# Delta-rule attention and two MLPs on one core: a reordered triangular solve on VectorE, a third high-word buffer, and a later first coupling in the second group

## The chip, the cores and the metric

One core of a Trainium2 chip runs the whole program. The metric is the device time of one execution in microseconds (us). Five engines take their own instruction queues in order: TensorE (PE in the rows, PEld for its weight loads), VectorE (DVE), ScalarE (ACT), GpSimd (POOL), and SyncE (SP), which here only issues DMA transfers. Engines meet through semaphores; an instruction whose wait is not fulfilled holds everything behind it on its own engine.

## The reference, cut to what matters

Attention is a recurrence with a state of 48 x 48 for each of 32 pairs of batch and head; behind it stand two MLPs on the same 4 x 768 tokens.

```python
def _attn_ref(q, k, v, beta):              # (4, 8, 768, 48) each, beta without the last axis
    k_n = k / (norm(k, axis=-1, keepdims=True) + 1e-06)
    for t in range(S):                     # S = 768
        y[:, :, t] = q[:, :, t] @ state
        v_old = state^T k_n[:, :, t]
        state = state + beta_t * outer(k_n[:, :, t], v[:, :, t] - v_old)

def _moe_ref(x, w_in, g_ln, w_sg, b_sg, w_out):
    h = gelu(x @ w_in)                     # 384 -> 1024
    u, v = h[..., :512], h[..., 512:]
    v_n = layernorm(v) * g_ln
    v_s = einsum('ts,bsd->btd', w_sg, v_n) + b_sg[None, :, None]
    return x + (u * v_s) @ w_out

def _moe2_ref(x, mu_k, mu_r, w_k, w_v, w_r):
    xk, xr = mixes of x and the token before
    return sigmoid(xr @ w_r) * (relu(xk @ w_k)**2 @ w_v)
```

## The kernel before

**Chunks and groups.** The 768 tokens are cut into 12 chunks (`s`) of 64, and two chunks make one of six groups (`g`, counted from 0). Inside a chunk the recurrence becomes a triangular system. PE makes the products of the keys with each other (`gram`), VectorE inverts the two 32 x 32 diagonal blocks of all 32 (chunk, pair) systems of a group at once (`solver(g)`, lanes are partitions), and PE makes from the inverses `DT` and the block under the diagonal `GL` the coupling of the two halves (`couple(g, k)`, one call for each chunk k of the group).

**The steps of a chunk** run on PE in two halves `o` of the pairs: `st_rq` (keys times state), `residual` (values minus that; ACT in group 0, VectorE in all others), `st_d` (the residual times the inverses `DT`, into `rk`), `st_n` (its product, copied as `u1`, times the coupled `GL`), `st_s` (state), `st_y` (output). `st_d` needs the solve and the residual; only `st_n` needs the coupling. Each half-chunk is one slot, each slot has three ticks, a group has 24 ticks.

**The solve** is one chain on VectorE: a transpose, a reciprocal norm (some 20 small instructions), the scaling of four 8 x 8 blocks (L389), a forward substitution inside the 8 x 8 blocks (pairs of a product, L355, and a sum, L393), the joining of 8 x 8 blocks to 16 x 16, and of these to 32 x 32 (again products of 256 to 1024 elements for a partition, each followed by its sum), and a transpose into `DT` (L440). Every product writes the same scratch tile `tmp`, so a product waits for the sum before it, and the sum for the product. `solver(g + 1)` runs while group g is on PE; the next one starts when the group changes.

**Weights in two words.** `w_in`, `w_out` and `w_k` are split into a high and a low word by `narrow` jobs: four VectorE instructions for each piece (L169, L171, L173, L175, on tiles `na` and `raw`), then POOL L177, an ACT copy L120 (the high word), POOL L123 (the low word). A new piece's L169 waits until an `na` buffer is free, which is after L123 of the piece that had it; there are `NNA` = 2 of them.

**What sets the order.** A planner in Python deals out VectorE's work at each tick (`background`) among three kinds: layer norm, solve, jobs, in the ratio `SHARE` (row 1 of the table is for group 0). PE, ACT, VectorE and POOL run the order in which the code is written; PE fills time with matmuls on a tile `warm` (L726) and with the input projection of the MLP (`v_units` L635, `u_units` L687). SP's order is set by the framework. Once the attention is through, PE goes on with the spatial mix (L960) and the products behind it (L151); `begin_early` loads `w_sg` for that mix in pairs of blocks ahead of time, one of them into a staging tile `stw`, through which later pieces of `w_sg` also pass.

Of the kernel before, what the change touches and what calls it, by code (L numbers as in the profile page):

```python
# [7 lines left out]
F32 = mybir.dt.float32  # L8
# [4 lines left out]
ALU = mybir.AluOpType  # L13
# [47 lines left out]
SHARE = ((1, 12, 1), (1, 4, 1), (2, 8, 2))  # L61
NRAW = 3
NNA = 2
# [23 lines left out]
def fused_kernel(  # L87
# [161 lines left out]
    with ExitStack() as at:  # L249
# [101 lines left out]
        def product(a_off, a_dims, a_t, b_off, b_dims, b_t):  # L351

            sh = [d[1] for d in a_dims]
            tv = vw(tmp, 0, [(sh[1] * sh[2], sh[0]), (sh[2], sh[1]), (1, sh[2])])
            V.tensor_tensor(tv, vw(a_t, a_off, a_dims), vw(b_t, b_off, b_dims), op=ALU.mult)  # L355
            return tv, sh[0] * sh[1] * sh[2] / 960 + 0.16

        def solver(g):
# [28 lines left out]
            for m in range(4):  # L387
                blk = NT[:, 8 * m:8 * m + 8, 8 * m:8 * m + 8]
                V.tensor_tensor(blk, blk, vw(c, 8 * m, [(1, 8), (0, 8)]), op=ALU.mult)  # L389
                yield 0.15  # L390
# [5 lines left out]
            for i in range(1, 8):  # L396
# [7 lines left out]
            yield 0.3  # L404
            for dst in (0, 1):
                for p in range(2):
                    o = 16 * p
                    if dst == 0:
                        tv, t = product(32 * (o + 8) + o, [(32, 8), (0, 8), (1, 8)], NT,
                                        128 * p, [(0, 8), (8, 8), (1, 8)], Yt)  # L410
                        ov = vw(NT, 8 + 528 * p, [(1, 8), (32, 8)])
                    else:
                        tv, t = product(33 * (o + 8), [(32, 8), (0, 8), (1, 8)], Dm,
                                        8 + 528 * p, [(0, 8), (32, 8), (1, 8)], NT)
                        ov = vw(Dm, 32 * (o + 8) + o, [(32, 8), (1, 8)])
                    yield t
                    yield total(ov, tv, t)
                    if dst and p == 0:
                        V.tensor_copy(vw(NT, 24, [(1, 8), (32, 8)]), ov)
                        yield 0.2  # L420
            for last in (0, 1):
                if last == 0:
                    ops = [(vw(Yt, 16 * j, [(1, 16), (16, 4)]),
                            (32 * 16 + j, [(32, 16), (0, 4), (1, 16 - j)], NT,
                             16 + 33 * j, [(0, 16), (32, 4), (1, 16 - j)], NT))
                           for j in (12, 8, 4, 0)]
                else:
                    ops = [(vw(Dm, 32 * (16 + i), [(32, 4), (1, 16)]),
# [824 lines left out]
```

## Time and profile before

| | us |
|---|---|
| median of 3 runs | 744.63 (743.13 to 745.2) |
| the profiled execution, time | 746.13 |
| its span | 744.3 |
| PE busy | 689.7 (93%) |
| VectorE busy | 506.3 (68%) |
| ACT busy | 364.8 (49%) |
| POOL busy | 202.5 (27%) |

The span is the time between the first and the last record; some 1.8 us lie around it. The page's chain of waits, followed back from the end, gives PE 67% of the span and VectorE 20%; of VectorE's part the largest lines are L355 (products of the solve, 5%) and L393 (their sums, 3% and 2%). TensorE's granted clock has a mean of 0.975 of full speed; in the rows 1.00 is 2.4 GHz and 0.50 is 1.2 GHz.

### The profile page before, as it was taken

What the parts mean: (1) busy time and instruction counts of PE and PEld (TensorE: products, weight loads), DVE (VectorE), ACT (ScalarE), POOL (GpSimd) and SP (SyncE); (2) the same over time, 40 slices, a digit from 0 to 9 for tenths busy, and PEclk for the clock granted to TensorE, in tenths of its full rate; (3) what the DMA queues carried; (4) which work ended last, traced back from release to release, by engine and by line L of the source; (5) the groups of instructions that cost most, each with busy time, mean ns of one, the idle gap of its engine ahead of it and who ended that gap; (6) DMA issues with size and microseconds to landing.
All of it is one profiled execution on the core that took longest, in us unless ns stands there. A gap on an engine that the chain in (4) does not pass through costs nothing.

```text
span 744.3 us, 24530 instructions
## 1 busy us (share of the span) xinstructions
PE 689.7 (93%) x10688; PEld 622.4 (84%) x10688; DVE 506.3 (68%) x1014; ACT 364.8 (49%) x696; POOL 202.5 (27%) x253
## 2 busy tenths in 40 slices
PE   3459789998998999899999999999999999999998
PEld 3337568887886987779999999998989899999997
DVE  5989999897888796642566857598656464736251
ACT  3226656776676676774331413146445453626140
POOL 3033544454345255463131515330000000000000
PEclk9968989999999899999999999999999999999999
DMA  8502443675556566848763545259000000000000
GB/s 237 133 29 86 126 102 94 165 215 160 138 178 165 148 182 172 231 144 226 245 222 106 168 153 168 85 193 232 23 21 22 22 21 22 11 33 11 32 11 33
DMA packets 81547, 88.72 MB, mean 119 GB/s; under 512 B 24704, under 2 KB 64320, under 8 KB 81440
## 3 DMA queue, kind: packets, MB, share of 16 engines
q1 hardware_dynamic: 76384, 77.72, 35.3%
q0 software_dynamic: 5056, 9.44, 4.8%
q8 instruction: 84, 1.38, 0.7%
q14 instruction: 23, 0.19, 0.1%
HBM read 56.60 MB, written 25.82 MB: 111 GB/s over the span
## 4 chain that ended last, share of the span: by engine, by line
PE 67%; DVE 20%; issue 4%; DMA 4%; POOL 2%; ACT 2%; SPq 0%; POOLq 0%; ACTq 0%; DVEq 0%
PE ms L151 34%; PE ms L960 11%; PE ms L687 5%; DVE sg L355 5%; PE ms L635 4%; DVE sg L393 3%; PE ms L563 2%; PE ms L456 2%; PE sps L549 2%; DVE Yt L393 2%; PE rk L521 1%; PE ms L333 1%; PE rk L534 1%; PE rk L498 1%; DMA raw<-in_w_k_dram 1%
## 5 line engine op out<-in xcount | busy, mean ns | idle before, releaser
L151 PE MATMUL ms<-wvh,sl 128*128 128x384 f32 x192 | 64.7, 337 | 0.5 <-DVE sl L123 0.5
L151 PE MATMUL ms<-wvh,sh 128*128 128x384 f32 x192 | 64.6, 337 | 0.1
L151 PE MATMUL ms<-wvl,sh 128*128 128x384 f32 x192 | 64.5, 336 | 0.0
L1059 ACT ACTIVATE gh<-w 128x384 fp32r<-128x384 f32 x32 | 16.8, 526 | 93.8 <-DVE w L1058 93.8
L177 POOL TENSOR_TENSOR na<-na,raw 128x256 int32<-128x256 int32 (+2 forms) x43 | 35.9, 835 | 96.2 <-ACT gh L1059 40.7
L151 PE MATMUL ms<-xm_hi,sw0h 128*128 128x512 f32 x144 | 56.1, 390 | 0.0
L151 PE MATMUL ms<-xm_hi,sw0l 128*128 128x512 f32 x144 | 56.1, 389 | 0.0
L151 PE MATMUL ms<-xm_lo,sw0h 128*128 128x512 f32 x144 | 56.0, 389 | 0.0
L123 DVE TENSOR_TENSOR sl<-sg,sh 128x512 fp32r<-128x512 f32 x48 | 33.2, 692 | 28.8 <-ACT sh L120 28.7
L960 PE MATMUL ms<-sw0h,g 128*128 128x384 f32 x192 | 50.2, 335 | 0.0
L960 PE MATMUL ms<-ws1h,g 128*128 128x384 f32 x192 | 49.9, 334 | 0.0
L120 ACT ACTIVATE sh<-sg 128x512 fp32r<-128x512 f32 x48 | 30.3, 631 | 34.0 <-DVE sg L1172 34.0
L1189 DVE TENSOR_TENSOR sg<-sg,ms 128x384 f32<-128x384 f32 x24 | 13.3, 553 | 49.3 <-PE ms L151 49.3
L355 DVE TENSOR_TENSOR sg<-sg,Yt 128x512 f32<-128x512 f32 (+10 forms) x78 | 45.6, 584 | 1.7
L514 POOL TENSOR_SCALAR_AFFINE_SELECT SQ<-SQ 64x512 f32<-64x512 f32 x36 | 27.9, 774 | 50.2 <-ACT SQ L513 49.0
L1171 ACT ACTIVATE sg<-ms 128x512 f32<-128x512 f32 x48 | 28.6, 595 | 26.1 <-PE ms L151 24.1
L1172 DVE TENSOR_TENSOR sg<-sg 128x512 f32<-128x512 f32 x48 | 33.2, 692 | 10.8 <-ACT sg L1171 10.8
L687 PE MATMUL ms<-xl,wiu_hi 128*128 128x256 f32 x144 | 39.5, 296 | 0.0
L687 PE MATMUL ms<-xh,wiu_hi 128*128 128x256 f32 x144 | 38.4, 289 | 0.8 <-issue 0.8
L687 PE MATMUL ms<-xh,wiu_lo 128*128 128x256 f32 x144 | 38.5, 290 | 0.0
L151 PEld LDWEIGHTS ms<-wvh,sl 128*128 128x128 f32 x192 | 36.1, 188 | 0.8 <-DVE sl L123 0.8
L393 DVE TENSOR_REDUCE sg<-sg 128x64 f32<-128x512 f32 (+3 forms) x48 | 35.9, 748 | 0.9
(246 smaller groups left out, 2155.5 us busy)
## 6 DMA issues: line engine op xcount, KB each, us to landing
u_d<-ug SPq DMA_DIRECT2D x24, 256.0 KB, 3.9
u<-u_d SPq DMA_DIRECT2D x16, 384.0 KB, 4.9
vn_d<-v SPq DMA_DIRECT2D x22, 256.0 KB, 3.3
vk<-in_vk_dram SPq DMA_DIRECT2D x24, 192.0 KB, 3.7
vk<-in_vk_dram SPq DMA_DIRECT2D x12, 384.0 KB, 4.5
out_dram<-sg SPq DMA_DIRECT2D x24, 192.0 KB, 1.9
kT<-in_kt_d_dram SPq DMA_DIRECT2D x8, 512.0 KB, 4.5
SQ<-in_q_d_dram SPq DMA_DIRECT2D x36, 96.0 KB, 3.6
```

What stands on the lines that cost most here:

```text
L120: A.activation(hi, src, AF.Copy)
L123: eng_lo.tensor_tensor(lo, src, hi.bitcast(F32), op=ALU.subtract)
L151: T.matmul(pt, lhsT=a, rhs=b, start=(i == 0), stop=(i == n - 1))
L177: G.tensor_tensor(a.bitcast(I32), a.bitcast(I32), w_lo.bitcast(I32), op=ALU.add)
L355: V.tensor_tensor(tv, vw(a_t, a_off, a_dims), vw(b_t, b_off, b_dims), op=ALU.mult)
L393: V.tensor_reduce(out=o_ap, in_=tv, axis=AX.X, op=ALU.add)
L514: G.affine_select(out=pt, in_=pt, pattern=[[0, 8], [1, C]], compare_op=ALU.is_gt, fill=0.0, base=0, channel_multiplier=-1)
L635: T.matmul(vstat[g, b], lhsT=a[:, c], rhs=w[:, c], start=first, stop=last)
L687: T.matmul(vstat["u"][:, 2 * P * d:2 * P * d + 2 * P], lhsT=w[:, c, ds_], rhs=a[:, c].rearrange("p b t -> p (b t)"), start=first, stop=last)
L960: T.matmul(pt[:, :DM], lhsT=v[:, ds_], rhs=w, start=(c == 0 and i == 0), stop=(c == 5 and i == 2))
L1171: A.activation(r, pt, AF.Relu)
L1172: V.tensor_tensor(r, r, r, op=ALU.mult)
```

## The change

Five things are changed.

1. **The solve's instructions.** The four scalings become one of 4 x 8 x 8; the first substitution step, which sums one element, becomes one product without a sum; the joins take two or three products and their sums in turn, in separate parts of `tmp` (offset `at`).
2. **The second group's couplings** are put at tick 27 and 33 or later: behind `st_d`, `st_s` and `st_y` of the slot in which the first one stood ahead.
3. **The second solve** (during group 0) starts at tick 0 instead of 1, and gets 8 parts to 1 of the jobs' instead of 4 to 1.
4. **`NNA`** is 3.
5. **The tile `stw`** is gone, which makes room for the third `na`: pair 1 of `w_sg` is loaded into the key buffer `kTb[2]`, and the first later piece passes through a tile `st0` of the mix's own pool.

```diff
-SHARE = ((1, 12, 1), (1, 4, 1), (2, 8, 2))
+SHARE = ((1, 12, 1), (1, 8, 1), (2, 8, 2))
-NNA = 2
+NNA = 3
...
-        def product(a_off, a_dims, a_t, b_off, b_dims, b_t):
+        def product(a_off, a_dims, a_t, b_off, b_dims, b_t, at=0):
-            tv = vw(tmp, 0, [(sh[1] * sh[2], sh[0]), (sh[2], sh[1]), (1, sh[2])])
+            tv = vw(tmp, at, [(sh[1] * sh[2], sh[0]), (sh[2], sh[1]), (1, sh[2])])
...
-            for m in range(4):
-                blk = NT[:, 8 * m:8 * m + 8, 8 * m:8 * m + 8]
-                V.tensor_tensor(blk, blk, vw(c, 8 * m, [(1, 8), (0, 8)]), op=ALU.mult)
-                yield 0.15
+            blk = vw(NT, 0, [(264, 4), (32, 8), (1, 8)])
+            V.tensor_tensor(blk, blk, vw(c, 0, [(8, 4), (1, 8), (0, 8)]), op=ALU.mult)
+            yield 0.4
+            V.tensor_tensor(vw(Yt, 1, [(64, 4)]), vw(NT, 32, [(264, 4)]), vw(Yt, 0, [(64, 4)]),
+                            op=ALU.mult)
+            yield 0.15
...
-            for i in range(1, 8):
+            for i in range(2, 8):
...
+            def pairs(ops, hooks={}):
+
+                for k, (x, e) in enumerate(ops):
+                    ov, args, at = e
+                    if x == "*":
+                        tvs[at], t = product(*args, at=at)
+                        yield t
+                    else:
+                        yield total(ov, tvs[at], 0.16 + args[1][0][1] * args[1][1][1] * args[1][2][1] / 960)
+                    if k in hooks:
+                        hooks[k]()
...
+                yield from pairs([("*", es[0]), ("*", es[1]), ("+", es[0]), ("+", es[1])])
...
+                    yield from pairs([("*", a), ("+", a), ("*", b), ("*", d), ("+", b), ("*", c_),
+                                      ("+", d), ("+", c_)])
...
+                    yield from pairs([("*", c_), ("*", d), ("+", c_), ("*", b), ("+", d), ("+", b),
+                                      ("*", a), ("+", a)], hooks)
...
                 p += -p % 6 if p % 6 > 2 else 0
+                if g == 1:
+                    p = max(p, 27)
                 for k in range(2):
                     later.append((p + 6 * k, lambda k=k: couple(g, k)))
...
-                streams.append([point[0] + SOLVE0, solver(g + 1), "solve"])
+                streams.append([point[0] + (SOLVE0 if g else 0), solver(g + 1), "solve"])
...
-                  1: fetch_pair(stg.tile([P, 2, DM], F32, name="stw", bufs=1), 1)}
+                  1: fetch_pair(vw(kTb[2], 0, [(DM, 2), (1, DM)]), 1)}
...
-                    st[2] = fetch_pair(stg.tile([P, 2, DM], F32, name="stw", bufs=1), 2)
+                    st[2] = fetch_pair(st[1], 2)
...
-    sts += [(stg, "stw"), (vr, "st1"), (vr, "st2")]
+    sts += [(vr, "st0"), (vr, "st1"), (vr, "st2")]
```

How this moves instructions is not told by the diff alone. In the rows below the line numbers of after are some 2 to 17 higher (L393 is L395, L440 is L455, L475 is L492, L456 is L473, L521 is L538, L726 is L743).

VectorE, from the end of the first solve to the start of the second: `sw0l` is the first solve's `DT`, `m_sb` a small constant. Before:

```order
L440 STREAM_TRANSPOSE sw0l_115<-sg_110 128x32x32
L175 SCALAR_TENSOR_TENSOR na<-raw,na 128x256
L827 TENSOR_SCALAR m_sb<-mu_sb 128x6
L169 TENSOR_SCALAR na<-raw 128x256 x2
L171 TENSOR_SCALAR na<-na 128x256 x2
L173 TENSOR_SCALAR na<-na 128x256 x2
L360 STREAM_TRANSPOSE sg_108<-sg_109 128x1024
```

And after, from the last product of the first solve on:

```order
L355 TENSOR_TENSOR sg_111<-sg_110,Yt 128x1024
L175 SCALAR_TENSOR_TENSOR na<-raw,na 128x256
L395 TENSOR_REDUCE sg_110<-sg_111 128x4x16
L455 STREAM_TRANSPOSE sw0l_115<-sg_110 128x32x32
L175 SCALAR_TENSOR_TENSOR na<-raw,na 128x256
L844 TENSOR_SCALAR m_sb<-mu_sb 128x6
L360 STREAM_TRANSPOSE sg_108<-sg_109 128x1024
```

Six instructions of two pieces have left the place between the two solves. Inside the second solve stand 12 instructions of pieces instead of 21.

VectorE, from the end of the second solve (`DT`) over the second group's first residual (`r`) to the third solve (L360). Before:

```order
L440 STREAM_TRANSPOSE DT<-sg_110 128x32x32
L169 TENSOR_SCALAR na<-raw 128x256
L175 SCALAR_TENSOR_TENSOR na<-raw,na 128x256
L475 TENSOR_TENSOR r_1642<-vk,rk 128x384
L171 TENSOR_SCALAR na<-na 128x256
L173 TENSOR_SCALAR na<-na 128x256
L175 SCALAR_TENSOR_TENSOR na<-raw,na 128x256
L360 STREAM_TRANSPOSE sg_108<-sg_109 128x1024
```

After, from the fourth instruction behind the transpose `L455 ... DT` on (the first three are L175, L171, L173):

```order
L175 SCALAR_TENSOR_TENSOR na<-raw,na 128x256
L169 TENSOR_SCALAR na<-raw 128x256 x2
L171 TENSOR_SCALAR na<-na 128x256 x2
L173 TENSOR_SCALAR na<-na 128x256 x2
L492 TENSOR_TENSOR r_1626<-vk,rk 128x384
L175 SCALAR_TENSOR_TENSOR na<-raw,na 128x256 x2
L169 TENSOR_SCALAR na<-raw 128x256
L171 TENSOR_SCALAR na<-na 128x256
L173 TENSOR_SCALAR na<-na 128x256
L360 STREAM_TRANSPOSE sg_108<-sg_109 128x1024
```

Between the transpose and the residual stand 14 instructions of pieces where there were two, and five more stand between the residual and the third solve, where there were three.

PE at the start of group 1. Before, the coupling (L456) stands ahead of `st_d` (L521):

```order
L726 MATMUL ms<-warm 128x512
L456 MATMUL ms<-DT,sw0h_113 32x32 x32
L726 LDWEIGHTS warm
...
L521 MATMUL rk<-r_1642,DT 32x48 x32
L549 MATMUL sps_104<-SQ_127,vk 48x48
```

After, `st_d` (L538), `st_s` (L566) and `st_y` (L580) come first, and `st_n` (L551) follows the coupling (L473):

```order
L743 MATMUL ms<-warm 128x512
L538 MATMUL rk<-r_1626,DT 32x48 x32
L566 MATMUL sps_104<-SQ_127,vk 48x48
...
L743 MATMUL ms<-warm 128x512
L473 MATMUL ms<-DT,sw0h_113 32x32 x32
L743 LDWEIGHTS warm
...
L551 MATMUL rk<-u_1731,sw0h_113 32x48 x16
```

The number of matmuls is the same. On SP the loads of `raw` have moved too: the last piece of `w_in` is now loaded behind six stores of attention output (`xT<-yst`, L600 and L605):

```order
L605 DMA xT<-yst 32x2x128
L160 DMA raw<-in_w_in_dram 128x512
L279 DMA SQ_127<-in_q_d_dram 48x8x64
L279 DMA SQ_128<-in_q_d_dram 48x8x64
L273 DMA vk<-in_vk_dram 64x768
```

Before, two pieces of `w_out` stood there:

```order
L588 DMA xT<-yst 32x2x128
L160 DMA raw<-in_w_out_dram 128x384 x2
L273 DMA vk<-in_vk_dram 64x768
L279 DMA SQ_127<-in_q_d_dram 48x8x64
L279 DMA SQ_128<-in_q_d_dram 48x8x64
```

That piece's L169 is the one that stands between the residual and the third solve.

## Rows read from the trace of the kernel before

**Rows 1.** Busy time by engine, 340 us to the end: PE, PEld, DVE, ACT, POOL, clock.

```profile
340.00:744.00 404.00, 400.28 (x2172) 380.80 (x2170) 233.58 (x400) 157.30 (x283) 54.24 (x55) 1.00 0.30 92
```

**Rows 2.** Waits of PE: total us, times, longest.

```profile
PE ms L726 <- DVE warm L435: 8.4, 1, 8.4
...
PE ms L456 <- DVE na L169: 4.7, 1, 4.7
PE ms L456 <- DVE sw0l L440: 3.8, 2, 3.6
```

**Rows 3.** Timeline of PE: start, duration, line, count, idle time before and releaser.

```profile
96.07 1.92 PE L456 MATMUL ms<-DT,sw0h 32*32 32x32 f32 x64 [4.70 <-DVE na L169]
...
104.65 0.87 PE L534 MATMUL rk<-u,sw0h 32*32 32x48 f32 x32
...
192.46 1.20 PE L456 MATMUL ms<-DT,sg 32*32 32x32 f32 x64 [1.56 <-DVE DT L440]
```

**Rows 4.** Busy time by engine behind the 4.70 us wait; the clock is 0.50.

```profile
96.00:102.50 6.50, 6.43 (x164) 4.89 (x164) 6.05 (x20) 2.50 (x5) 3.40 (x5) 0.50 0.27 73
```

**Rows 5.** Timeline of VectorE in the first solve.

```profile
22.42 0.49 DVE L389 TENSOR_TENSOR sg<-sg,c 128x64 f32<-128x64 f32 x3
...
29.08 0.69 DVE L355 TENSOR_TENSOR sg<-sg,Yt 128x512 f32<-128x512 f32 x1
29.80 0.69 DVE L393 TENSOR_REDUCE sg<-sg 128x64 f32<-128x512 f32 x1
30.41 0.28 DVE L171 TENSOR_SCALAR na<-na 128x256 f32<-128x256 f32 x1
...
33.59 0.42 DVE L355 TENSOR_TENSOR sg<-sg 128x256 f32<-128x256 f32 x1
```

**Rows 6.** Timeline of VectorE between the first and the second solve.

```profile
49.56 0.40 DVE L175 SCALAR_TENSOR_TENSOR na<-raw,na 128x256 uint32<-128x256 uint32 x1
...
52.09 0.29 DVE L169 TENSOR_SCALAR na<-raw 128x256 uint32<-128x256 uint32 x1 [1.88 <-POOL wiv_lo L123]
...
54.04 1.23 DVE L360 STREAM_TRANSPOSE sg<-sg 128x1024 f32<-128x1024 f32 x1
```

**Rows 7.** Timeline of VectorE behind the second solve, and the third solve's start.

```profile
95.77 0.28 DVE L169 TENSOR_SCALAR na<-raw 128x256 uint32<-128x256 uint32 x1
...
98.09 1.24 DVE L360 STREAM_TRANSPOSE sg<-sg 128x1024 f32<-128x1024 f32 x1
```

**Rows 8.** Groups of VectorE in the second solve: busy us and mean ns.

```profile
L169 DVE TENSOR_SCALAR na<-raw 128x256 uint32<-128x256 uint32 x5 | 3.0, 592 | 0.0
...
L173 DVE TENSOR_SCALAR na<-na 128x256 uint32<-128x256 uint32 x6 | 1.9, 324 | 0.0
```

**Rows 9.** Timeline of POOL: one piece and the start of the next.

```profile
96.50 0.73 POOL L177 TENSOR_TENSOR na<-na,raw 128x256 int32<-128x256 int32 x1 [1.84 <-issue]
...
98.72 0.73 POOL L177 TENSOR_TENSOR na<-na,raw 128x256 int32<-128x256 int32 x1
```

**Rows 10.** Timeline of VectorE: the last residual of group 1.

```profile
133.45 0.56 DVE L475 TENSOR_TENSOR r<-vk,rk 128x384 f32<-128x384 f32 x1 [2.14 <-PE qk L501]
```

**Rows 11.** Timeline of SP's queue, and landing times of the loads of `raw`.

```profile
92.56 1.30 SPq L583 DMA_DIRECT2D xT<-yst  x2
93.92 2.63 SPq L588 DMA_DIRECT2D xT<-yst  x4
...
DMA to landing us min/median/max: 2.4/2.9/4.0
```

**Rows 12.** ACT, PE and SP's queue behind the attention, and a load's landing time.

```profile
343.11 0.60 ACT L644 ACTIVATE v<-ms 128x512 f32<-128x512 f32 x1 [4.84 <-PE ms L635]
...
349.26 0.86 PE L635 MATMUL ms<-wiv_hi,xh 128*128 128x512 f32 x3
...
341.50 0.90 SPq L243 DMA_DIRECT2D st<-in_w_sg_dram  x2
...
st<-in_w_sg_dram SPq DMA_DIRECT2D x2, 192.0 KB, 4.3
```

More of the change, by code (lines that the diff above doesn't have):

```diff
@@ L404, in solver @@
             yield 0.3
+            def pairs(ops, hooks={}):
[8 more added lines that the diff above has]
+                        hooks[k]()
+            tvs = {}
             for dst in (0, 1):
+                es = []
                 for p in range(2):
@@ L416, in solver @@
[L416 to L420, printed above, removed]
+                        es.append((vw(NT, 8 + 528 * p, [(1, 8), (32, 8)]),
+                                   (32 * (o + 8) + o, [(32, 8), (0, 8), (1, 8)], NT,
+                                    128 * p, [(0, 8), (8, 8), (1, 8)], Yt), 512 * p))
+                    else:
+                        es.append((vw(Dm, 32 * (o + 8) + o, [(32, 8), (1, 8)]),
+                                   (33 * (o + 8), [(32, 8), (0, 8), (1, 8)], Dm,
+                                    8 + 528 * p, [(0, 8), (32, 8), (1, 8)], NT), 512 * p))
@@ L421, in solver @@
+                yield from pairs([("*", es[0]), ("*", es[1]), ("+", es[0]), ("+", es[1])])
+            V.tensor_copy(vw(NT, 24, [(1, 8), (32, 8)]), es[0][0])
+            yield 0.2
             for last in (0, 1):
                 if last == 0:
[L423 to L426, printed above, removed]
-                else:
-                    ops = [(vw(Dm, 32 * (16 + i), [(32, 4), (1, 16)]),
-                            (32 * (16 + i) + 16, [(32, 4), (0, 16), (1, i + 4)], Dm,
-                             0, [(0, 4), (16, 16), (1, i + 4)], Yt)) for i in (0, 4, 8, 12)]
@@ L431, in solver @@
-                for i, (ov, args) in enumerate(ops):
-                    tv, t = product(*args)
-                    yield t
-                    if g == 0 and last and i == 1:
-                        V.memset(warm, 0.0)
-                    if g == 0 and last and i == 2:
-                        scale_v(0)
-                    yield total(ov, tv, t)
+                    es = [(vw(Yt, 16 * j, [(1, 16), (16, 4)]),
+                           (32 * 16 + j, [(32, 16), (0, 4), (1, 16 - j)], NT,
+                            16 + 33 * j, [(0, 16), (32, 4), (1, 16 - j)], NT), at)
+                          for j, at in ((0, 0), (4, 0), (12, 768), (8, 0))]
@@ new lines, in solver @@
+                    a, b, d, c_ = es
+                    yield from pairs([("*", a), ("+", a), ("*", b), ("*", d), ("+", b), ("*", c_),
+                                      ("+", d), ("+", c_)])
+                else:
+                    es = [(vw(Dm, 32 * (16 + i), [(32, 4), (1, 16)]),
+                           (32 * (16 + i) + 16, [(32, 4), (0, 16), (1, i + 4)], Dm,
+                            0, [(0, 4), (16, 16), (1, i + 4)], Yt), at)
+                          for i, at in ((4, 0), (0, 768), (8, 0), (12, 0))]
+                    c_, d, b, a = es
+                    hooks = {2: lambda: V.memset(warm, 0.0), 3: lambda: scale_v(0)} if g == 0 else {}
+                    yield from pairs([("*", c_), ("*", d), ("+", c_), ("*", b), ("+", d), ("+", b),
+                                      ("*", a), ("+", a)], hooks)
```

6 lines of the change are left out of this document (removed).

## The prediction, made blind

> **What bounds the kernel now.** I read the busy times by stretch first. From 340 us on PE is busy 400.28 of 404.00 us at full clock [rows 1], and the change touches little there: what is saved ahead of 340 us should arrive at the end nearly whole. So I read PE's waits ahead of 340 us next. The long ones are for VectorE's solves: 8.4 us ahead of the first solve's end, 4.7 us at the coupling of group 1 behind the second, and 3.8 us in two waits behind a later one, 3.6 of them in one [rows 2]. The timeline shows the 4.7 us wait ending at 96.07, with the product `st_n` it was for at 104.65, and a third such wait of 1.56 us at 192.46 [rows 3]. Behind the 4.7 us wait the granted clock is 0.50, which is 1.2 GHz: the coupling there takes 1.92 us and in rows 3 also 1.20 [rows 3, 4]. So this wait costs more than itself.
>
> **The first solve (whole on the path).** The row to read is how soon the next instruction starts. A product of 512 elements at 29.08 is followed by its sum, which waits for it, after 0.72 us; the sum at 29.80 is followed by an instruction that does not wait after 0.61 [rows 5]. A direct wait costs 0.11 us. Behind the substitution, the code before has 18 instructions that wait for the one directly ahead of them, the code after 5: 13 x 0.11 = 1.4 us. Three of four scalings, at some 0.13 us each, make way for longer work of 256 elements: a tile operation of that size is busy 0.42 us [rows 5], less an overlap of 0.09 with the next, so 0.5 becomes 0.3; the sum that falls away and the two direct waits beside it I take for 0.3, an estimate from the small instructions in these rows. Together 1.9 to 2.0 us.
>
> Against this stands a rule of the Trainium skill (VectorE: DVE Perf Modes, The DRAIN you can't avoid): every VectorE operation is followed by a flush of its pipeline, which ordering or leaving out semaphores does not save. By that the 1.4 us would not be there and the first solve would give 0.5. Rows 5 speak for 0.11 a pair; what the rule would make of the time is rival 3.
>
> **The second solve.** Its start moves from 54.04 to about 48.0: the instruction behind the first solve, at 49.56, comes 2.0 earlier, and six instructions of pieces with their 1.88 us wait for POOL no longer stand ahead of L360 [rows 6]. Its length was 95.77 - 54.04 = 41.7 us [rows 6, 7]. It loses nine instructions of pieces. The means of these in that stretch are 0.324 to 0.592 us [rows 8]; less 0.09 overlap that is 2.1 to 4.5, and I take 3.8, near the upper end since what falls away is work that VectorE and POOL did at the same time. Its own instructions save only 0.7, since pieces already stood between many of its pairs (36 direct waits before, 32 after). So it ends at about 48.0 + 41.7 - 4.5 = 85.2, with bounds of 83.5 and 87 against 95.8.
>
> **What is late next: the residual.** The coupling no longer waits; `st_d` needs the residual, and 14 instructions of pieces now stand ahead of that on VectorE. At 0.3 us each they take 4.3. But the last two L169 need `na` buffers that POOL frees, and POOL takes 2.2 us from one piece to the next (96.50 to 98.72) [rows 9]; two such pieces, behind the 0.4 us of the first L175, make the second buffer free at about 4.8 us behind the solve, and five more instructions follow. So the residual starts 6.2 us behind the solve (bounds 4.3 and 7.2), at 91.4, and is through at 91.9. PE comes to that place 4.7 us ahead of 96.07, at 91.4, less the 2.0 of the first solve, so at 89.4 [rows 3]. It waits about 2.5 us there: the old wait is halved, not gone.
>
> From `st_d` to `st_n` stand the pieces that stood from the coupling to `st_n` before, in another order: 104.65 - 96.07 = 8.6 us at half clock. At full clock I take 6.2 (8.6 less 6.5 us of rows 4 at a saving of 0.72 of 1.92). A wait of 1.56 us was followed by a lower clock in part, so I take 7.0. `st_n` then starts at 91.9 + 7.0 = 98.9 instead of 104.65: **5.7 us**, with bounds of 2.5 and 9.
>
> **What takes part of it back: the third solve.** It starts at 98.09 now [rows 7]. The last piece of `w_in` stands ahead of it, and its load now stands on SP behind six stores of output, 1.30 + 2.63 us of issuing [rows 11]. These wait for an ACT copy that stands behind another piece; I put its end at 89.1, so the load is issued at 93.1, lands after 2.4 to 4.0 us, median 2.9 [rows 11], and three instructions later the third solve starts at 96.9 (bounds 95 and 98.5), 1.2 us earlier. Up to group 1's last residual it saves some 0.7 of its own time. There VectorE waited 2.14 us for PE [rows 10]. So VectorE can follow PE by 1.2 + 0.7 + 2.14 = 4.0 us, not by 5.7. Some tenths of slack lie between that residual and its user on PE. I take **4.2 us** for groups 0 and 1.
>
> **The later groups.** From group 2 on, only VectorE's work behind the last residual counts, since ahead of it VectorE waits for PE as at 133.45. Counting the instructions there with the 0.11 us: group 1's last stretch has one more, -0.2; the wait of 1.56 shrinks by 0.5; that of 3.6 by 0.9. Together **+1.2**. Spells of half clock behind these two waits may shorten too, by up to 1.4 us each as I scale the coupling's 1.92 to 1.20; I leave them out of the sum and in the range.
>
> **The third buffer and the staging tile.** The third `na` takes away the waits of L169 for buffers and adds no instruction. Without `stw`, the first piece of `w_sg` behind the attention is loaded where `st` is now, at 341.50 [rows 12]. It lands 4.3 us later, so at about 345.5, and the ACT copy in front of the work that ACT began at 343.11 holds that until 346. ACT was idle 4.84 us before it. PE needs the product of that chain at 349.26 [rows 12], with about 3 us of work in between: **-0.4**, bounds 0 and -2. Pair 1 goes into a key buffer whose last use is long past; I cost it at nothing.
>
> **The sum.** 4.2 + 1.2 - 0.4 = 5.0 us against the profiled execution's 746.13 us gives 741.1. That execution is 1.5 us above the median of 744.63, so the time by the median is 739.6; I say 739.5.
>
> **Rivals.**
> 1. *More: nothing but PE bounds groups 0 and 1.* If the pieces ahead of the residual take 4.3 us, the solve ends at 83.5 and the load lands early, `st_d` stands at 89.4 and runs at full clock: `st_n` at 95.6, 9 us earlier. With 1.2 and part of the half-clock spells this gives 734 to 736. For it: POOL has less to do. Against it: rows 9 and 11 each cap it alone.
> 2. *The third solve eats more.* If the load lands after 4.0 us behind stores that start late, the third solve starts at 98.5, and VectorE follows by 2.4 only. With 1.2 - 0.4 the time is 741.4, with a longer residual up to 743.4; I put it at 742.
> 3. *Reordering saves no time, only the merged scalings do* (the rule above). The first solve gives 0.5, the second ends 1.9 us later, the third starts 0.7 later than now with 0.2 saved. VectorE then follows by 2.14 - 0.7 + 0.2 = 1.6, the later groups give nothing, and the time is 744.63 - 1.6 + 0.4 = 743.4. Rows 5 speak against it.
> 4. *The gain is given back:* a new wait of ACT in group 0. In front of a copy `u1` on ACT now stand two copies of high words, which need two L175 in the middle of the second solve. If these come 4 to 5 us later than PE does, the 5 us are gone: 744 to 745.
> 5. *Slower: the load at the attention's end.* The copy from `st0` stands on ACT in front of all of the projection's work. It costs nothing up to a landing at 346, then 1 us for each us. From a landing at 351 on it eats the 5.0 us, and from 353.2 the time is over 746.9; in a stretch where loads and stores share the queue this could be 748. Against it: 4.3 us for such a load in rows 12; it would need 12.
>
> **How the numbers follow.** The forecast of 739.5, with its own range of 737.6 to 741.4, gets 0.50; rival 1 (below 737.6) 0.15; rival 2 0.15; rival 3 0.06; rival 4 0.06; rival 5 0.08. From 735 to 743 lie the forecast, most of rivals 1 and 2, 0.8 in all. A measurement of this kernel tells 0.3% (2.2 us) from no change, so faster means below 742.4 and slower above 746.9. Faster: 0.50 + 0.15 and half of rival 2, 0.73; slower: rival 5, 0.08; the rest, 0.19, is the same.
>
> **What would show each step.** In the changed kernel's trace: the second solve's transpose ends near 85 instead of 95.8, and sums that follow a product of another pair start 0.61 us behind a 512-element one; if they still stand at 0.72, rival 3 holds. `st_d` in group 1 waits for VectorE's residual (L492) for 2 to 3 us and no wait is left at the coupling; a wait under 1 us there speaks for rival 1. The third solve starts at 95 to 98, behind a wait of L169 for a load. `st_n` of group 1 starts near 99. The two later waits at the coupling are near 1.1 and 2.7 us. Behind the attention ACT waits for the load of `st0` to about 346 and PE has no wait of over 1 us. I would be wrong if a wait of PE over 3 us stands in group 0, or if group 1's gain is not found again at 340 us.

## The result, and the profile after

The changed kernel takes 750.51 us (median of 9 runs, 745.23 to 754.44) against 744.63 us for the kernel before: a ratio of 1.0068, 95% interval 1.0046 to 1.0090. It is **slower** by 0.5 to 0.9%, some 5 us, where 739.5 was forecast; the prediction had put its bound for slower at 746.9. Its profiled execution took 746.27 us (span 744.5), 4 us under its median, so beside it a second profile of the same kernel is read below (the run `e1_after_again`, 749.92 us, near the median).

From 340 us on nothing moved, as with [rows 1]. Busy time by engine:

```profile
340.00:744.00 404.00, 400.47 (x2173) 381.00 (x2171) 233.93 (x401) 157.24 (x284) 54.03 (x55) 1.00 0.30 93
```

PE's waits (total us, times, longest) stand at other places now. The 4.7 us at the coupling of [rows 2] are gone; waits for the residual L492 on VectorE, 1.2 us before (L475), are now 6.0 us in two pieces, and 9.6 us in the second profile:

```profile
PE rk L538 <- DVE r L492: 6.0, 2, 3.6
PE ms L743 <- DVE warm L451: 4.1, 1, 4.1
...
PE ms L473 <- DVE DT L455: 1.9, 1, 1.9
...
PE ms L473 <- DVE sw0l L455: 1.5, 1, 1.5
```

VectorE in the first solve: start, duration, line, count. The two products of a pair now follow each other, then their two sums. From 26.56 to 28.95 stand four of them, 0.60 us each; in [rows 5] a sum that waits for its own product came after 0.72. So the reordering does what it says: the first solve, up to the first instruction behind it, went from 33.79 us to 31.64.

```profile
26.56 1.29 DVE L355 TENSOR_TENSOR sg<-sg,Yt 128x512 f32<-128x512 f32 x2
27.76 1.27 DVE L395 TENSOR_REDUCE sg<-sg 128x64 f32<-128x512 f32 x2
28.95 0.28 DVE L171 TENSOR_SCALAR na<-na 128x256 f32<-128x256 f32 x1
```

The same view from the end of the second solve into the third, to be held against [rows 7]:

```profile
80.45 1.96 DVE L455 STREAM_TRANSPOSE DT<-sg 128x1024 f32<-128x1024 f32 x1
82.27 0.65 DVE L175 SCALAR_TENSOR_TENSOR na<-raw,na 128x256 uint32<-128x256 uint32 x1
...
83.16 1.55 DVE L173 TENSOR_SCALAR na<-na 128x256 uint32<-128x256 uint32 x1
...
86.87 0.84 DVE L175 SCALAR_TENSOR_TENSOR na<-raw,na 128x256 uint32<-128x256 uint32 x1
88.33 0.29 DVE L169 TENSOR_SCALAR na<-raw 128x256 uint32<-128x256 uint32 x1 [0.61 <-DMA raw<-in_w_in_dram]
91.21 0.29 DVE L169 TENSOR_SCALAR na<-raw 128x256 uint32<-128x256 uint32 x1 [2.59 <-POOL wiu_lo L123]
...
92.42 0.55 DVE L492 TENSOR_TENSOR r<-vk,rk 128x384 f32<-128x384 f32 x1
...
97.63 0.32 DVE L169 TENSOR_SCALAR na<-raw 128x256 uint32<-128x256 uint32 x1 [3.98 <-DMA raw<-in_w_in_dram]
...
98.52 1.24 DVE L360 STREAM_TRANSPOSE sg<-sg 128x1024 f32<-128x1024 f32 x1
...
110.18 0.55 DVE L492 TENSOR_TENSOR r<-vk,rk 128x384 f32<-128x384 f32 x1
```

The second solve ends 13.5 us earlier (82.27 for 95.77). Then the pieces that were pushed out of it, with two waits, take 10 us to the residual. There are 14 instructions of them; the listing under The change shows the last seven. The third solve starts at 98.52 against 98.09, and in the second profile at 101.43. The last row is the one I had not looked for: the **second residual of group 1** stands some 12 us inside the third solve, so it comes when that solve lets it. Before, it was done at 109.68 and PE used it at 112.54:

```profile
109.14 0.54 DVE L475 TENSOR_TENSOR r<-vk,rk 128x384 f32<-128x384 f32 x1
112.54 0.88 PE L521 MATMUL rk<-r,DT 32*32 32x48 f32 x64
```

Now PE waits 3.61 us for it:

```profile
93.03 1.50 PE L538 MATMUL rk<-r,DT 32*32 32x48 f32 x64 [2.37 <-DVE r L492]
...
99.07 1.20 PE L473 MATMUL ms<-DT,sw0h 32*32 32x32 f32 x64
...
110.78 0.88 PE L538 MATMUL rk<-r,DT 32*32 32x48 f32 x64 [3.61 <-DVE r L492]
...
117.00 1.20 PE L473 MATMUL ms<-DT,sw0h 32*32 32x32 f32 x64 [0.35 <-ACT yst L585]
```

Behind that stands a second new wait, on ACT. The first piece of `w_out` begins with a scaling on ACT (L164); its load now stands on SP behind the key load of group 2, at 108.63, where it stood at 90.82 before. SP's queue before (first row) and after, then ACT:

```profile
90.82 0.33 SPq L160 DMA_DIRECT2D raw<-in_w_out_dram  x1
...
91.19 2.58 SPq L605 DMA_DIRECT2D xT<-yst  x4
93.88 0.52 SPq L160 DMA_DIRECT2D raw<-in_w_in_dram  x1
...
108.16 0.38 SPq L267 DMA_DIRECT2D kT<-in_kt_d_dram  x1
108.63 1.32 SPq L160 DMA_DIRECT2D raw<-in_w_out_dram  x3
```

```profile
107.71 0.82 ACT L342 ACTIVATE sg<-ms 128x256 f32<-128x256 f32 x2
114.71 0.38 ACT L164 ACTIVATE raw<-raw 128x192 int32<-128x192 uint32 x1 [6.18 <-DMA raw<-in_w_out_dram]
114.99 0.47 ACT L543 ACTIVATE u<-rk 128x384 f32<-128x384 f32 x1
```

The copy `u` stands behind that wait, though PE had its input ready soon after 110.78. In the second profile the late residual alone sets `u`: ACT's wait for the load is 3.08 us, and behind it ACT waits another 1.59 us for the product of that residual, which PE began at 114.41:

```profile
114.07 0.38 ACT L164 ACTIVATE raw<-raw 128x192 int32<-128x192 uint32 x1 [3.08 <-DMA raw<-in_w_out_dram]
114.41 1.50 PE L538 MATMUL rk<-r,DT 32*32 32x48 f32 x64 [4.79 <-DVE r L492]
116.03 0.49 ACT L543 ACTIVATE u<-rk 128x384 f32<-128x384 f32 x1 [1.59 <-PE rk L538]
```

In the first profile the first `st_n` of group 1 starts at 101.25 (104.65 in [rows 3], 3.4 us gained) and the second at 122.13 (119.14 before, 3.0 us lost). The groups behind take some of it up: at the last `st_n` of the attention this execution is 0.16 us behind the one of before. In the second profile the second `st_n` stands at 125.49, 6.35 us late, of which 3.9 us are left at the last `st_n`.

At the attention's end, the load that replaces the staged one lands at 345.5, as forecast (346), and PE waits for nothing over 0.4 us there: from the last `st_n` to the end it is 411.9 us in both kernels. ACT:

```profile
345.48 0.53 ACT L120 ACTIVATE ws1h<-st 128x384 fp32r<-128x384 f32 x1 [7.47 <-DMA st<-in_w_sg_dram]
```

### The profile page after: what moved, and what is told of

It reads as the page before. It is cut to its first block, busy times and chain, and to the rows that moved or that the text cites. A ratio compares the mean times of both kernels' runs of the same rounds, so it can differ in the third digit from the quotient of the medians.

```text
span 744.5 us, 24490 instructions
## 1 busy us (share of the span) xinstructions
PE 689.5 (93%) x10688; PEld 621.4 (83%) x10688; DVE 499.7 (67%) x990; ACT 363.4 (49%) x696; POOL 201.5 (27%) x253
## 4 chain that ended last, share of the span: by engine, by line
PE 72%; DVE 12%; DMA 5%; issue 4%; POOL 3%; ACT 3%; SPq 1%; POOLq 0%; ACTq 0%; DVEq 0%
PE ms L151 34%; PE ms L977 11%; PE ms L704 6%; PE ms L652 6%; DVE sg L355 2%; PE ms L580 2%; PE rk L551 2%; PE rk L515 2%; DMA raw<-in_w_in_dram 2%; PE rk L538 2%; PE sps L566 2%; PE ms L473 1%; PE ms L333 1%; POOL na L177 1%; DMA wk_d<-raw 1%
## 5 line engine op out<-in xcount | busy, mean ns | idle before, releaser
L177 POOL TENSOR_TENSOR na<-na,raw 128x256 int32<-128x256 int32 (+2 forms) x43 | 38.2, 889 | 91.2 <-ACT gh L1076 40.7
L355 DVE TENSOR_TENSOR sg<-sg,Yt 128x512 f32<-128x512 f32 (+4 forms) x72 | 42.2, 593 | 1.4
L333 PEld LDWEIGHTS ms<-kT 64*32 64x32 f32 x640 | 18.7, 126 | 22.4 <-issue 14.0
```

The costliest lines, as they stand in the source:

```text
L177: G.tensor_tensor(a.bitcast(I32), a.bitcast(I32), w_lo.bitcast(I32), op=ALU.add)
L333: T.matmul(gps[r:r + 32, p, c0:c1], lhsT=t[r:r + 64, u, 0:32], rhs=t[r:r + 64, u, c0:c1], start=True, stop=True)
```

## The experiments

Theory A says that the pieces pushed behind the second solve cost the time (late residuals, a late third solve, late `w_out` loads). Theory B says the late coupling does. Theory C says the denser solve does. The runs come in five sets, each on one chip with the kernel before beside it, so ratios are compared rather than medians. "Stretch" is the time on PE from the last `st_n` of group 0 to the second of group 1, from each run's own timeline (88.23 to 119.14 before). It comes from one execution and is not the whole time: from there to the last `st_n` the profiles of all runs take between 208.0 and 222.2 us (213.3 before). The profiles of e3, e4, e6 and e11 lie 4.9, 3.8, 3.9 and 7.0 us above their medians, that of e13 3.5 us below.

| run | what it is | median us | ratio, 95% | third solve | second residual | stretch |
|---|---|---|---|---|---|---|
| before | | 744.63 | 1 | 98.09 | 109.14 | 30.9 |
| after | the change | 750.51 | 1.0046 to 1.0090 | 98.52 | 110.18 | 35.8 |
| e1 | the change again | 750.83 | 1.0021 to 1.0083 | 101.43 | 113.81 | 37.3 |
| e2 | change, coupling back | 751.69 | 1.0032 to 1.0079 | 100.65 | 113.02 | 36.4 |
| e3 | change, share 4 | 747.60 | 0.9984 to 1.0037 | 94.39 | 107.33 | 35.7 |
| e4 | before + reordering | 746.44 | 0.9965 to 1.0023 | 96.03 | 106.76 | 31.0 |
| e12 | before + third buffer | 744.73 | 0.9932 to 0.9986 | 94.55 | 107.79 | 25.9 |
| e6 | before + reordering + third buffer | 738.60 | 0.9827 to 0.9916 | 91.06 | 104.08 | 26.4 |
| e9 | e6 again | 742.14 | 0.9896 to 0.9944 | 90.96 | 103.98 | 25.6 |
| e10 | e6 + early second solve | 741.97 | 0.9907 to 0.9970 | 92.07 | 105.24 | 28.0 |
| e11 | e6 + share 8 | 749.50 | 1.0001 to 1.0051 | 100.86 | 113.36 | 33.3 |
| e13 | e6 + late coupling | 743.80 | 0.9938 to 1.0003 | 91.77 | 104.31 | 29.1 |

**The change again, and three parts undone.**

> The changed kernel as it is, a second time. The first 9 executions lay between 745 and 754 us, the kernel before between 742 and 747. If the scatter belongs to the kernel (a wait that is long in some executions, short in others), it is seen again: a median of 748 to 751 and a spread of over 5 us, and its profile shows which of the waits in group 1 has another length than in the first profile (2.4 us at the first residual, 3.6 us at the second, ACT 6.2 us behind a load of w_out). If it was that chip, the spread is 3 us and the median within 2 us of before.

The loss is there again, at a median of 750.83 us and with a spread of 10.5 us; 31 executions of the kernel before in the same set spread over 7.9 us. In group 1 it is the waits for the residual that are longer than in the first profile (3.49 and 4.79 us for 2.37 and 3.61).

`e2_couple_back` takes out of the changed kernel:

```diff
-                if g == 1:
-                    p = max(p, 27)
```

> The change with its second part undone: the couplings of group 1 stand ahead of their products again, all else as changed. Theory A (pieces of weights and their loads between the second and the third solve hold the residuals): the solve ends at about 82, so the coupling waits for nothing and fills 1 to 2 us of PE's wait for the residual; the second residual is still late and the time is 746 to 749. Theory B (the later coupling lengthens the chain behind the second product, where ACT is blocked): d to n of the second half takes 7 us as before instead of 11, the 3 us loss at 122 us is gone, and the time is 741 to 743.

751.69 us lies above both ranges. Undoing the late coupling alone gives nothing, so I dropped theory B here; too early, as e13 and, with e3, e10 suggest.

`e3_share4` has the old share:

```diff
-SHARE = ((1, 12, 1), (1, 8, 1), (2, 8, 2))
+SHARE = ((1, 12, 1), (1, 4, 1), (2, 8, 2))
```

> The change with the share of the second solve back at 4 to 1 (it still starts at tick 0; couplings late, three buffers, reordered solve): 22 instead of 12 instructions of pieces inside the second solve, six ahead of the first residual, four to the third solve. Theory A: the second solve ends near 89 to 90, the residual follows within 2 us, the third solve starts near 94 instead of 98.5, no wait for a load of the last piece, no 3.6 us wait at the second residual: 739 to 742. Theory B: the late coupling still costs 3 us: 744 to 747.

747.60 us is just above theory B's range. By the ratios that gives back 3 to 4 of the 4 to 5 us lost, though the intervals of e1 and e3 overlap; the stretch stays long, in an execution 4.9 us above the median.

`e4_reorder_only` is the kernel before with the new `solver` and `product` alone.

> Only the reordered solve; order of the pieces, couplings, two buffers and staging tile as before. Theory A and B both: the first solve ends 2.1 us earlier, the second 2.5 to 3 us, the waits at the coupling of later groups shrink by 0.5 and 0.9: 740 to 742. Theory C (the denser solve loses its gain to POOL or to waits for PE): 743.5 to 745.

It gives nothing that can be measured; 746.44 us lies above all the ranges. VectorE's trace suggests why. Its waits between 44 and 100 us were 1.9 us for POOL before; now they are 6.7: a solve that is through its own work sooner comes sooner to buffers that POOL has not freed:

```profile
DVE na L169 <- POOL wiu_lo L123: 4.8, 2, 2.6
DVE na L169 <- POOL wiv_lo L123: 1.9, 1, 1.9
```

The second solve has got longer by it (50.93 to 94.03, 43.1 us for 41.7), and PE's wait at the coupling stays at 4.23 us:

```profile
94.34 1.92 PE L471 MATMUL ms<-DT,sw0h 32*32 32x32 f32 x64 [4.23 <-DVE na L169]
```

**Which part pays.** `e6_reorder_third_buffer` adds to this the third buffer and the staging that goes with it, and nothing else (the staging lines are those of The change):

```diff
-NNA = 2
+NNA = 3
...
```

> The kernel before with the reordered solve, three high-word buffers and the staging taken away with them; share 4 to 1, the second solve's start and the coupling as before. Theory A (pieces pushed behind the second solve cost, the buffers do not): within 1 us of the reordered solve alone, 745.5 to 747.5, no wait of ACT over 1 us for the w_out load. If the third buffer itself costs (it lets VectorE's last step of a piece run ahead, and the load of st0 moves to the attention's end): 748.5 to 750. If it pays: below 745.

> The reordered solve with three buffers and nothing else of the change, a second time. Theory T (the third buffer takes VectorE's waits for POOL out of the second solve, 1.88 + 2.6 + 2.15 us of L169 in the reordered kernel with two, and with no piece pushed behind that solve the whole gain reaches the end): 738 to 741, ratio to before 0.985 to 0.993; no wait of PE at group 1's coupling over 1 us, and st_d and st_n there 5 to 7 us earlier than before. If the 738.6 was the luck of six runs: 743 to 746.

> The kernel before with three buffers alone (and the staging that goes with it); the solve in the old order. Theory T, as far as the buffers work by themselves: 742 to 744 (the waits of L169 for POOL go, the first solve's 3.1 us stay). If reordering and buffers help only together (either one's gain is taken up by the other's wait): 744.5 to 747.

`e9_third_buffer_again` is the same kernel again, `e12_third_buffer_alone` the kernel before with the buffer and its staging. e6 and e9 beat the kernel before and the changed one: 0.8 to 1.3% under the kernel before, 5.4 to 8.4 us by the medians of the two sets. The third buffer alone gives 2.9 us and the reordering alone nothing, so by the medians both together give more than the sum; the intervals do not settle that (e12 0.9932 to 0.9986, e9 0.9896 to 0.9944). By the medians e9 lies between its two ranges and e12 in the one for help only together; by the ratios e9 is inside theory T's range and e12 alone is faster than before. In e9 VectorE's waits in the same stretch are 1.0 us, none for POOL; the second solve takes 39.1 us, though all its pieces are still in it, and the coupling does not wait and runs at full clock (1.20 us for 1.92). VectorE's waits, its third solve and second residual, and PE:

```profile
DVE na L169 <- DMA raw<-in_w_in_dram: 1.0, 2, 0.5
```

```profile
90.96 1.24 DVE L360 STREAM_TRANSPOSE sg<-sg 128x1024 f32<-128x1024 f32 x1
103.98 0.55 DVE L490 TENSOR_TENSOR r<-vk,rk 128x384 f32<-128x384 f32 x1
```

```profile
90.18 1.20 PE L471 MATMUL ms<-DT,sw0h 32*32 32x32 f32 x64
```

`e10_start_early` has the second solve one tick earlier in addition.

> The same, but the second solve starts one tick earlier, in front of the three steps of pieces that stood there. Theory A (each step pushed behind the second solve comes back as a later third solve and as late weight loads): 741 to 745, between this kernel's parent and the changed kernel with share 4 (747.6). If an earlier solve is worth its 2 us at the coupling: 736 to 738.

The early start neither pays nor costs (0.9939 beside 0.9920 in the same set).

**Which part costs.** `e11_share8_only` is e6 with the share of 8 to 1, the diff of e3 the other way round.

> The reordered solve with three buffers and the share of 8 to 1; start and coupling as before. Theory A: 746 to 750, residuals of group 1 waited for by PE (L490 on VectorE) for 2 us or more each, the gain of 6.7 us at st_d lost by the second st_n. If only the three parts together do harm: 738 to 742.

As theory A said, it costs: 7.4 us against e9 in the same set, with intervals well apart. Its profiled execution is its longest (756.5), so it serves for the order of events in group 1 and not for sizes:

```profile
94.31 0.54 DVE L490 TENSOR_TENSOR r<-vk,rk 128x384 f32<-128x384 f32 x1
99.53 0.29 DVE L169 TENSOR_SCALAR na<-raw 128x256 uint32<-128x256 uint32 x1 [4.68 <-DMA raw<-in_w_in_dram]
100.86 1.24 DVE L360 STREAM_TRANSPOSE sg<-sg 128x1024 f32<-128x1024 f32 x1
113.36 0.55 DVE L490 TENSOR_TENSOR r<-vk,rk 128x384 f32<-128x384 f32 x1
```

The chain is seen from end to end here: a piece left over waits for a load that SP issues behind six stores, the third solve starts 9.9 us later than in e9, the second residual 9.4 us later, and the stretch is 7.7 us longer. That this chain makes the 7.4 us is not shown by it; see e14.

`e8_share6` has a share of 6 to 1 in the changed kernel.

> The changed kernel with the second solve shared 6 to 1 instead of 8 to 1. Theory A in steps (each piece that is pushed behind the second solve costs the same): between the share of 4 (747.6) and the share of 8 (750.8), 748.5 to 750. If it is one threshold (the piece on which the third solve or the w_out load waits), the median is that of one of the two, 747 to 748 or 750 to 752, and ACT's wait for the w_out load is either under 3 us or over 5.

752.63 us (1.0043 to 1.0102), third solve at 100.64: no step in between, but the full loss. That speaks for one threshold rather than a price for each piece, though ACT's wait for the `w_out` load was 3.83 us, between the two bounds that I had set.

`e13_late_couple_alone` is e6 with the late coupling.

> The reordered solve with three buffers (742.1 and 738.6 before) and the late coupling of group 1 in addition; share 4, start as before. Its first w_out load stands early on SP. If the late coupling costs by itself, as 747.6 against 742.0 with the early start and share 4 says (theory B'): second st_n of group 1 two to five us later than 112.7, median 744 to 748. If that difference was all ACT's wait for the w_out load (5.34 us there, absent here): 739 to 743.

0.9970 where e9 has 0.9920; 743.80 us lies between the two ranges, and the two intervals touch. The trace shows a cost at that place: PE waits 2.16 us for a copy ahead of the warming products, the clock is 0.50 from 99.8 to 106.6, and the second coupling stands right in front of the products that need it, at 112.73 instead of 100.97. The second `st_n` is 4.4 us later (117.05 for 112.69). But this execution makes it up behind that point (209.7 us to the last `st_n`, 214.8 in e9), so the trace puts no price on it.

```profile
99.14 1.28 PE L743 MATMUL ms<-warm 128*128 128x512 bf16 x4 [2.16 <-ACT yst L585]
...
112.73 1.20 PE L473 MATMUL ms<-DT,sw0h 32*32 32x32 f32 x64
```

e3 and e10 differ in the late coupling alone, and their ratios are 1.0010 (0.9984 to 1.0037) and 0.9939 (0.9907 to 0.9970): 5 us, with intervals just apart. So theory B holds where the share is 4. At a share of 8 nothing clear of noise shows it (e2 beside e1, and e15 beside e14 below); that its cost lies there in the shadow of the others is my reading, not shown.

`e7_all_but_reorder` is the changed kernel with the old solve.

> The changed kernel with the solve's instructions in the old order and number: three buffers, share 8, early start of the second solve, late coupling stay. Theory A (the loss is that of the pieces behind the second solve, and the reordering's 2 us are independent of it): the second solve ends 2.5 to 3.5 us later than in the changed kernel, group 1's st_n later by as much, and the median is 751 to 753. Theory C (the denser solve is what starves the pieces, so the loss needs both): the median falls back to 746.5 to 748.5.

751.67 us (1.0051 to 1.0102), as theory A says: the loss needs no denser solve. Theory C falls, and the reordering is worth nothing that shows there. The first `st_n` of group 1 comes 6.6 us later than in the changed kernel (107.80 for 101.25) and the second hardly later (123.34 for 122.13): what is gained ahead of the first is lost at the second.

**By which path the share costs.** Three waits were taken away in the changed kernel, alone and together.

`e5_jobs_later` moves ACT's scaling of the `w_out` piece behind the copies that it held up:

```diff
-                start_job(LJ5 if late else LJ)
+                start_job(LJ5 if late else LJ + 6 * (24 <= point[0] < 48))
```

> The changed kernel, but weight jobs started between ticks 24 and 48 get six ticks more lead, which moves ACT's first step of the w_out piece (the one that waited 6.18 us for its load in the changed kernel) behind the copies of u and v of the second half. Theory A1 (that wait of ACT, with the two waits of PE behind it, is what turns the 3.4 us gained at the first st_n of group 1 into 3.0 lost at the second): the wait is gone from ACT ahead of u, the second st_n of group 1 stands at 118 to 120 instead of 122.1, and the median is 2 to 4 us below the changed kernel's, at 746.5 to 748.5. Theory A2 (the residual inside the third solve, a PE wait of 3.6 to 4.8 us for L492, is the cause and ACT's wait lies in its shadow): st_n stays at 121 to 123 and the median at 749.5 to 752.

`e14_third_solve_first` starts the third solve in front of the last pieces:

```diff
-                streams.append([point[0] + (SOLVE0 if g else 0), solver(g + 1), "solve"])
+                streams.append([point[0] + (SOLVE0 if g > 1 else 0), solver(g + 1), "solve"])
```

> The changed kernel with one edit: the third solve is started one tick earlier, so its first instruction stands in front of the last piece of w_in on VectorE (three steps) instead of behind it. Theory A2 (the third solve's start, held by that piece's load, sets the second residual of group 1 some 12 us later, and PE waits for that): third solve at 93 to 95 instead of 98.5 to 101.4, second residual at 105 to 108, PE's waits there under 1 us, median 746 to 749. If the piece is not what costs: 750 to 752.

Neither moves the time: 750.42 us (1.0015 to 1.0072) and 751.41 us (1.0037 to 1.0102). So neither ACT's wait (A1) nor the late third solve (A2) is the cause by itself. In e5 ACT's wait is gone, but the third solve starts at 102.26, so the second residual is 4.7 us later than in the profile of after. The edit of e5 also has a price elsewhere: from the last `st_n` to the end it is 413.6 us for 411.9. In e14 the third solve starts at 92.88 and the second residual at 105.61, as A2 says, and PE waits 0.38 us for that one; the time of A2, 746 to 749, did not come. The wait for the first residual is still there (4.3 of the 4.7 us), and at the late coupling there is one for a copy that stands behind ACT's wait for the load (3.3 us). PE's waits from 88 to 125 us:

```profile
PE rk L538 <- DVE r L492: 4.7, 2, 4.3
PE ms L473 <- ACT yst L585: 4.4, 1, 4.4
```

`e15_third_solve_first_couple_back` has the edits of e14 and e2.

> The run before with the coupling put back as well; the share of 8 and the early second solve remain. If late third solve and late coupling are the two causes and add up (A2 and B'): 741 to 744, near the reordered solve with three buffers. If the w_out loads behind the key load on SP are a third cause that stays: 745 to 748.

`e17_and_jobs_later` has those of e14, e2 and e5.

> The share of 8 to 1 and the early second solve, with the third solve first, the coupling back (749.4) and now the first step of the w_out piece on ACT moved behind the copies it held up by 3.09 us. If the w_out load behind the key load is the third cause: that wait is gone from ACT ahead of v, PE's 1.01 us at L333 with it, the stretch from the last product of group 0 to the second st_n of group 1 falls from 29.4 to 26 to 28 us, and the median is 742 to 746. If the share of 8 costs somewhere later: the stretch is short but the median stays at 747 to 750.

e15 takes 749.43 us (0.9995 to 1.0055), above both its ranges, with a stretch of 29.4 us; e17 takes **743.14 us** (0.9933 to 0.9990), at a stretch of 30.9. For e17 the time came as the first half of the expectation says, the stretch did not. ACT shows that the wait in that place only changed its cause:

```profile
111.09 0.38 ACT L164 ACTIVATE raw<-raw 128x192 int32<-128x192 uint32 x1 [3.09 <-DMA raw<-in_w_out_dram]
```

```profile
111.29 0.42 ACT L120 ACTIVATE wiu_hi<-na 128x256 fp32r<-128x256 f32 x1 [4.38 <-POOL na L177]
```

The first row is e15, the second e17; ACT goes on at the same time in both. So the 6 us between these two are not won in group 1. In their profiles they lie behind it: from the second `st_n` of group 1 to the last of the attention e15 takes 218.9 us and e17 210.3. The granted clock of 116.5 to 335 us is 0.97 and 0.99 there, but over the 12 executions of each run its mean is 0.977 in both, so half clock does not explain the medians. PE also waits longer in e15 for nothing that the profile shows (7.3 us in all for 4.0). One profile of each cannot settle whether that follows from where the pieces stand. It **stays open**. What the two runs show is that a share of 8 need not cost 7 us.

`e18_share4_third_solve_first` is e15 with a share of 4.

> The same with the share of 4 to 1 instead (no change to the jobs' lead): early second solve, third solve first, coupling back. All causes found are undone, so 740 to 743 and a stretch of 26 to 28 us; 746 or more would say that a cause has been missed.

741.28 us (0.9908 to 0.9955), stretch 26.7: as expected. Against e15 it is the share alone, and the intervals are apart, as with e11 and e9.

`e16_buffers_third_solve_first` is e6 with the third solve a tick earlier.

> The reordered solve with three buffers, and the third solve one tick earlier. There only two steps stand in front of it and none of them waits over 0.6 us, so A2 says little is to be had: 741 to 743.5, no difference from the run without. If it is below 740, the third solve was late there too.

740.20 us (0.9884 to 0.9947), just under the range: no difference from e9 that can be told; there the third solve was not late.

## Why the prediction was wrong

1. **First solve: right on VectorE, not carried on by PE.** 2.0 us were forecast, VectorE gained 2.15. The rule that I took from the Trainium skill (VectorE: DVE Perf Modes, The DRAIN you can't avoid), that leaving out waits saves no time, does not hold here: 0.60 us a step for 0.72. The same section of the Trainium skill also says that a next operation that is not held starts earlier, and 0.60 us is in line with that. But the last `st_n` of group 0 came at 86.31 in one profile and at 88.24 in the other (88.23 before), so the 2.0 us that I took into group 1 were there once and not the second time. And e4 shows them alone to be worth nothing that can be measured: VectorE's waits for POOL's buffers grow by 4.8 us there. I had set the 1.88 us of [rows 6] down as a wait that goes, and not asked what a faster solve does where the buffers stay.
2. **Second solve: better than forecast.** It starts at 47.24 (48.0) and ends at 82.27 (85.2, bounds 83.5 to 87).
3. **First residual: a term mis-sized.** 6.2 us behind the solve were taken, bounds 4.3 and 7.2; it was 10.2. Single instructions of the pieces took 0.84 and 1.55 us where I had used 0.3, and besides POOL's buffers (2.59 us) a load was waited for (0.61). The first `st_n` came at 101.25, and at 103.68 in the second profile, where 98.9 was forecast: 3.4 and 1.0 us gained for 5.7.
4. **What the pushed pieces hold up: the step that failed.** The prediction let the pieces behind the second solve cost PE some 2.5 us at the residual, and then let the gain through to the end of group 1 but for what the third solve takes: 4.2 us for groups 0 and 1. Measured, the second `st_n` of group 1 is 3.0 and 6.35 us *later* than before, and the share of 8 that pushes the pieces costs 7.4 us (e11 beside e9). The third solve was put at 96.9, bounds 95 and 98.5, and started at 98.52 and 101.43, behind waits of 3.98 and 4.63 us for a load that SP issued at 93.88 and 96.14 (93.1 forecast). And I took the *last* residual of group 1 [rows 10] as the place where VectorE and PE meet again. The *second* residual, inside the third solve, comes sooner, and its slack before was 2.9 us. With the third solve later than before instead of 1.2 us earlier, the gain ahead could not pass that point whole. But this is not the only such place: with the third solve at 92.88 (e14) the time stayed at 751.41 us. Points 5 and 6 name two more; how the 7 us divide among them stays open, as e17 shows.
5. **The pieces: looked for on two engines out of four.** That a third buffer "adds no instruction" was true, but pieces that come later on VectorE free their `raw` buffers later, so the next weight's loads move on SP, from 90.82 to 108.63, and ACT, whose first step of a piece waits for its load, stands for 6.18 us ahead of `u` in the first profile. I followed SP's queue for the last `w_in` piece and not for the next weight.
6. **The late coupling was taken as free.** "The pieces that stood from the coupling to `st_n` before, in another order" left out that the second coupling moves too, in front of its product. By the ratios e3 beside e10 puts 5 us on that and e13 beside e9 4 us, both at a share of 4, and the intervals of the second pair touch.
7. **Later groups and the end.** +1.2 us was forecast. From the second `st_n` of group 1 to the last of the attention the two profiles gain 2.8 and 2.4 us; PE's waits for VectorE at the later couplings shrink from 6.3 us to 3.4 and 2.9. Both a shorter solve and a PE that comes later shorten them, and no run tells the two apart. Behind the attention nothing was gained (0.4 forecast).

The rivals had one slower case, a load at the attention's end, which did not come. Rival 4's wait in group 0 did come in part: PE waited 1.74 and 0.84 us for `u` at the last `st_n` there (0.53 before). A second residual or a next weight's load that comes late was not among them. The forecast size, 5 us, is about what the reordering and the third buffer give without the rest (e9); that the sizes agree is luck, since the forecast's 4.2 us for groups 0 and 1 were to come with the pieces pushed back.

## What to carry to other kernels

Where work is taken out of a wait's way and put behind it, follow it on every engine that has a step of it, its loads included, up to the next place where the waiting engine needs something from each; each such place can cap the gain, not the last alone. A shorter chain on an engine that shares buffers with a slower one may need the buffers too: by the medians neither edit alone gave what both did together. And an edit undone alone can show nothing while other waits stand beside it, as with e2, e5 and e14: judge parts by adding them to the kernel before as well as by taking them from the kernel after.

## What the runs showed of the hardware

PE stood still in the middle of a series of products for which the profile shows nothing to wait for. In group 0 the 64 products of the second `st_d` break between the 33rd and the 31 that follow, at the same place in the program in before (0.87 us), after (0.69 us), e4 (1.97 us) and e9. PE in e9:

```profile
60.10 0.56 PE L536 MATMUL rk<-r,sw0l 32*32 32x48 f32 x33
62.84 0.54 PE L536 MATMUL rk<-r,sw0l 32*32 32x48 f32 x31 [2.17 <-issue]
```

The profile names no cause, and no run here was made for it. Such waits can eat part of what the first solve gains before group 0 is over: in e4 its first `st_n` comes 3.1 us earlier than before (53.27 for 56.39) and its last only 1.3 us (86.97 for 88.23), and this break is 1.1 us of the difference.
